# Float64 weights converted without a clamp and range-checked in a second pass, with a plan that takes transfers in the order of asking

## The chip, the cores and the metric

The kernel runs on one core of one Trainium2 chip. The metric is the device time of one execution in microseconds; lower is better. One profiled execution of the kernel before is at hand, with its trace.

## The reference

An attention block feeds a feed-forward block. For 4 batches, 8 heads, 768 steps and a head size of 48:

```python
f = 1.0 / (1.0 + np.exp(-f_logit))
for t in range(S):
    state = f[:, :, t, :, None] * state + np.einsum('bhd,bhe->bhde', k[:, :, t], v[:, :, t])
    y[:, :, t] = np.einsum('bhd,bhde->bhe', q[:, :, t], state)
x = y.transpose(0, 2, 1, 3).reshape(3072, 384)
a = x @ w1          # w1, w2: 384 x 1024
b = x @ w2
h = a * b @ w3      # w3: 1024 x 1024
out = h @ w_out     # w_out: 1024 x 384
```

q, k, v and f_logit are float32. The four weights are float64: `randn` in float32 times a Python-side `1/np.sqrt(n)`, which is a float64 number. So each weight is two 32-bit words, and the kernel makes float32 numbers of them on the chip.

## The kernel before

**Units and blocks.** The 3072 tokens are 24 units of 128 steps (6 for each batch). A unit's attention is a chunk: sigmoid gates on ACT, two scans on DVE (`fwd`, line 388, and `bwd`, line 410), the products K (418) and Q (404) on DVE, pair products on PE, a causal select on POOL (571), values and state on PE. The first four units (`u < NPE`) have a form of their own that uses PE fully for 128 steps; from unit 4 on a "visit" of PE does the values of unit u together with the pairs of unit u+1 (lines 515, 441, 534, 548). Four units make a block of 512 tokens for the feed-forward part, so there are six blocks. A unit's output `ys` (710) goes into the block's `xt`: for the first four units by PE (739, 744), for later ones through DRAM, written as `yt` (731) and gathered into `xt` (734).

**Feed-forward.** w3 @ w_out is folded into one matrix `wc` first: eight folds of 16 PE matmuls each (line 1221), copied by ACT (1228). Block 0 and half of block 1 multiply x by w1 and w2 plainly (`part`: copy `ab` on ACT, 798; product on DVE, 803). The rest uses a block product of seven multiplications (`seven`): m1, m6, m5, m2, m7, m4, m3 on PE, the copy k1 (tile `a`, line 864) of m1's result on ACT, sums on DVE (885 to 903). The down product does the same (line 997 for its sums, 1004 and 1017 for its copies on ACT). All feed-forward matmuls are issued in `three`, line 761. DVE makes differences of the weights once (1253, 1267) and of a block's xt (831).

**Weights.** `fetch` (from line 1109) loads a piece of float64 weights (line 1138) into one of a few places of the tile `place` and converts it in `sub`. With hi and lo the two words of a number:

- ACT, 1157: m = |hi|, as float32
- ACT, 1160: lo times 2^-51 plus 2, which leaves rounded bits of lo
- DVE, 1163: m clamped between LOW and HIGH
- DVE, 1164: m shifted left by 3
- DVE, 1168: sign bit of hi, or-ed with lo's bits
- DVE, 1174: the sum of the two

The clamp sends a number outside float32's useful range to an end of it. There are 12 pieces of w1 and w2 (512 columns), 4 of w_out (768), 8 of w3 (1024). A new piece may be loaded only when the DVE operation of 1168 has read the one that held the place.

**What sets the order.** Nothing is scheduled at run time. `Plan` collects tasks (engine, cost, dependencies, priority) and `order` lays them out by a list schedule: of the tasks that can start, the one that starts earliest, then the one with the lower priority number. The instructions are emitted in that order, so each engine's queue has a fixed order, and an instruction that waits holds what stands behind it. A transfer is two tasks: an issue on SP (0.45) and a task of an engine "DMA" (size over rate), made by `moves` (329). In spans where the plan sees PE idle in the first 35 us, `idle` (268) puts in filler matmuls on `floor`.

**The end.** `judge` (DVE) looks at the smallest of the gates' products and whether all outputs are numbers; the verdict goes through DRAM (1291, 1295) into the word `left`. Each engine reads it just before PE's last matmul group and, if it is set, a slower general program runs behind. For these inputs it is not set.

Of the kernel before, what the change touches and what calls it, by code (L numbers as in the profile page):

```python
# [36 lines left out]
F32 = mybir.dt.float32  # L37
# [30 lines left out]
HIGH = float.fromhex("0x1.dffffep+16")  # L68
W = C // 2
FULL = 35.0  # L70
FLOOR = 2.0**-60
RANGE = 2.0**-40


class Plan:
# [15 lines left out]

    def add(self, eng, cost, emit, deps=(), prio=0.0, takes=(), frees=(), lag=0.2, slack=0.0):


        t = {
            "eng": eng, "cost": cost, "emit": emit, "deps": [d for d in deps if d is not None], "prio": prio,
            "takes": list(takes), "frees": list(frees), "lag": lag, "slack": slack, "at": None, "end": None, "no": len(self.tasks),
        }
        self.tasks.append(t)
        return t  # L100

    def order(self):
        free, done, left = {}, [], list(self.tasks)
        enders = {}
# [15 lines left out]
        def start(t):  # L120

            waits, at = list(t["deps"]), free.get(t["eng"], 0.0)
            for name in t["takes"]:
                if name in self.pools:
                    ends = places(t, name)
                    if not ends:
                        return None
                    at = max(at, min(ends)[0])
                    continue
                n, taken = self.slots[name]  # L130
                if len(taken) >= n:
                    waits += enders[id(taken[-n])]
            ready = after(t, waits)
            return None if ready is None else max(at, ready)

        while left:
            at, _, _, t = min(
                ((at, t["prio"], t["no"], t) for t in left if (at := start(t)) is not None), key=lambda x: x[:3]
            )
            t["at"], t["end"] = at, at + t["cost"]  # L140
            free[t["eng"]] = t["end"]
            for name in t["takes"]:
                if name in self.pools:
                    t["got"] = min(places(t, name))[1]
                    self.pools[name][t["got"]] = t
                else:
                    self.slots[name][1].append(t)
            left.remove(t)
            done.append(t)
# [4 lines left out]
def kernel(  # L154
# [19 lines left out]
    with tc.manual_schedule():  # L174
        outside = ranged(tc, q, k, f_logit, v, w1, w2, w3, w_out, out, ident, w12, wc, left)
        with tc.If(outside > 0, preferred_fallthrough_block=True, label="general"):
            general(tc, q, k, f_logit, v, leaf_mask, out, ident, w12, wc)

# [6 lines left out]
def place_of(jc):  # L185

    return jc % KH * 2 + jc // KH
# [7 lines left out]
def ranged(ctx, tc, q, k, f_logit, v, w1, w2, w3, w_out, out, ident, w12, wc, left):  # L195
# [16 lines left out]
    floor = keep.tile([R, NQ], F32, name="floor")  # L212
    back = keep.tile([R, NQ], F32, name="back")
    gate = [keep.tile([R, NQ + 1], F32, name=f"gate{i}") for i in range(2)]
    qs, ks, fs = ([keep.tile([R, NQ], F32, name=f"{nm}{i}") for i in range(n)] for nm, n in (("q", 3), ("k", 2), ("f", 2)))
    masked = [keep.tile([P, 2, HP, C], F32, name=f"A{i}") for i in range(2)]
    flat = [t.rearrange("p r h c -> p (r h c)") for t in masked]
    diag = [t[:, 0 : 2 * HP * W].rearrange("p (r h c) -> p r h c", r=2, h=HP) for t in flat]
# [109 lines left out]

    def moves(n, size, rate, emit, deps, prio, late=0.0):


        for j in range(n):
            i = plan.add("SP", 0.45, (lambda: None) if j else emit, [d] if j else deps, prio - j * 1e-3, takes=["lane"], lag=0.6)
            d = i
            t = plan.add("DMA", size / n / rate, lambda: None, [i], prio - j * 1e-3, lag=1.3 + late, frees=[i])
        return t
# [5 lines left out]
    def front(u):  # L342
# [22 lines left out]

        t["lf"] = moves(2, 197, 250, load(fu, f_logit), free(2, "g"), n0 - 30)
        t["lk"] = moves(2, 197, 250, load(ku, k), free(2, "k"), n0 - 29.5)
        t["lq"] = moves(2, 197, 250, load(qu, q), free(3, "q"), n0 - 29)

# [35 lines left out]

        t["q"] = plan.add("DVE", 0.7, scale_q, [t["p"], t["lq"]] + past(u, 3, "v", "a"), n0 + 0.1)

# [11 lines left out]

        t["k"] = plan.add("DVE", 0.7, scale_k, [t["r"], t["lk"]] + past(u, 2, "a", "t"), n0)  # L420
        if u in (2, 3):
# [208 lines left out]
    def rest(u):  # L630
# [119 lines left out]
        else:  # L750
            t["z"] = moves(2, 197, 250, written, [t["y"]], n0 - 100)
            t["x"] = moves(1, 197, 250, gathered, [t["z"]] + before, n0 - 100)

# [355 lines left out]
    def fetch(loads_, a, prio, subs, deps=()):  # L1109
# [29 lines left out]

        ld = moves(1, total, 380, load, held, prio, max(0.0, 3.5 - 1.2 * load_no) if load_no < 4 * KM else 3.0)  # L1140
        asked.append(ld)
# [4 lines left out]
        def sub(c0, c1, dst, due, waits):  # L1146
# [8 lines left out]

            def magnitude():
                nc.scalar.activation(m, hi.bitcast(F32), AF.Abs)  # L1157

            def rest():
                nc.scalar.activation(lo.bitcast(F32), lo, AF.Copy, bias=2.0, scale=2.0**-51)  # L1160

            def shifted():
                nc.vector.tensor_scalar(m, m, HIGH, LOW, ALU.min, ALU.max)
                nc.vector.tensor_scalar(m.bitcast(U32), m.bitcast(U32), 3, None, ALU.logical_shift_left)

# [9 lines left out]

            past = [joins[i] for i in mine if i in joins]
            b = plan.add("ACT", 0.2 + 0.43 * w, magnitude, [ld] + past, due)
            e = plan.add("ACT", 0.2 + 0.43 * w, rest, [ld], due)
            h = plan.add("DVE", 0.32 + 0.54 * w, shifted, [b], due)
            g = plan.add("DVE", 0.16 + 0.53 * w, signed, [e, b] + list(waits), due)  # L1180
            j = plan.add("DVE", 0.16 + 0.53 * w, joined, [h, g], due - 1)
# [92 lines left out]
    where = {}  # L1274

    def judge():
        low = work.tile([R, 1], F32, name="low")
# [5 lines left out]
        nc.vector.tensor_scalar(nil, nil, 0.0, None, ALU.is_equal)  # L1283
        good = work.tile([R, 1], F32, name="good")
        nc.vector.tensor_scalar(low, low, RANGE, None, ALU.is_ge)
        nc.vector.tensor_tensor(good, low, nil, ALU.mult)
        where["good"] = good

    def told():
        where["all"] = dram.tile([R, 1], F32, name="good")  # L1290
        nc.sync.dma_start(where["all"], where["good"])

    def heard():
        row = work.tile([1, R], F32, name="row")
        nc.sync.dma_start(row, where["all"].rearrange("r one -> one r"))
        where["row"] = row
# [7 lines left out]
    for u in range(NU):  # L1304
# [11 lines left out]
        if u == NU - 1:  # L1316
            looked = plan.add("DVE", 1.0, judge, [tk[i]["y"] for i in range(NU)], -20)
            sent = moves(1, 0.4, 250, told, [looked], 0, 20.0)
            judged = plan.add("DVE", 0.2, decided, [moves(1, 0.4, 250, heard, [sent], 0, 20.0)], -20)
# [3 lines left out]
    for t in plan.order():  # L1323
# [6 lines left out]
        t["emit"]()  # L1330
    return blk[NB - 1]["outside"]


# [335 lines left out]
```

## Time and profile before

| | us |
|---|---|
| median of 3 runs | 477.67 (477.29 to 477.99) |
| the profiled execution, its own time | 482.72 |
| its span, first to last instruction | 481.0 |
| PE busy | 468.7 |
| DVE busy | 362.8 |
| ACT busy | 141.1 |
| POOL busy | 62.5 |
| mean granted clock of PE | 0.995 |

The durations used below come from the profiled execution, which took 5.05 us more than the median of the runs. The page has busy times of each engine, the span in 40 slices, the chain of work that ended last, and the costliest groups of instructions. A share of busy time is an average over stages with different limits; the views by stage and the waits say where an engine was held and by what. In the lists of waits a row reads: engine and line that waited, what released it, total us, times, longest. In the groups it reads: line, engine, operation, output from input, shape, count, then busy us and mean ns of one, then idle time before it.

PE's instruction list has one entry for a float32 matmul; the profile shows two rows for it.

### The profile page before, as it was taken

To read this page: it belongs to the slowest core of one execution; us is meant where nothing else is said; L and a number is where in the kernel's file an instruction comes from. 1 tells how busy PE (TensorE), PEld (TensorE's weight loads), DVE (VectorE), ACT (ScalarE), POOL (GpSimd) and SP (SyncE) were. 2 spreads that over 40 slices of the span, in tenths; PEclk is the share of its full clock that TensorE was granted. 3 is DMA by queue.
4 is the path that set the end of the run, shared out by engine and by line. 5 is a ranking of instruction groups with operands and counts; after the bars stand their busy time and mean duration, and the time that the engine had idled before them with its cause. 6 is when DMAs were issued, how large, how long until landed. Compare 5 with 4: busy or idle time off the path is not lost.

```text
span 481.0 us, 11341 instructions
## 1 busy us (share of the span) xinstructions
PE 468.7 (97%) x4667; PEld 400.4 (83%) x4667; DVE 362.8 (75%) x706; ACT 141.1 (29%) x310; POOL 62.5 (13%) x88
## 2 busy tenths in 40 slices
PE   8899999999999899999999999999999999999996
PEld 7788644656799688889988889988899888889995
DVE  7999699999999689899999567357653667664541
ACT  4697456462313334432432110001100110110000
POOL 9300000013303133312422100000000000000000
PEclk9999999999999899999999999999999999999999
DMA  6899277743415566446531002000111000000011
GB/s 183 269 387 236 54 278 246 260 138 100 134 50 162 163 172 169 115 132 169 148 110 46 18 18 65 34 33 2 34 33 58 9 0 1 0 1 1 34 66 37
DMA packets 36618, 50.10 MB, mean 104 GB/s; under 512 B 4546, under 2 KB 26050, under 8 KB 35538
## 3 DMA queue, kind: packets, MB, share of 16 engines
q1 hardware_dynamic: 36562, 49.33, 33.6%
q8 instruction: 37, 0.61, 0.6%
q14 instruction: 19, 0.16, 0.1%
HBM read 40.67 MB, written 8.65 MB: 103 GB/s over the span
## 4 chain that ended last, share of the span: by engine, by line
PE 73%; DVE 13%; DMA 6%; POOL 3%; issue 2%; ACT 1%; SPq 1%; DVEq 0%; POOLq 0%; ACTq 0%
PE f L761 62%; DVE place L1168 2%; PE f L1221 2%; DMA place<-in_w_dram 2%; PE py L515 2%; DVE place L1174 2%; DMA place<-in_w_out_dram 2%; PE f L455 2%; PE pa L441 2%; PE pa L548 2%; PE py L534 1%; DMA f<-in_f_logit_dram 1%; SPq L1138 1%; POOL ab L306 1%; DVE place L1253 1%
## 5 line engine op out<-in xcount | busy, mean ns | idle before, releaser
L761 PE MATMUL f<-xt,w 128*128 128x256 f32 (+1 forms) x600 | 162.8, 401 | 3.2 <-ACT gate L380 2.0
L761 PEld LDWEIGHTS f<-xt,w 128*128 128x128 f32 x600 | 114.1, 192 | 29.5 <-issue 10.0
L761 PE MATMUL f<-place 128*128 128x192 f32 (+1 forms) x504 | 112.1, 349 | 0.1
L761 PEld LDWEIGHTS f<-place 128*128 128x128 f32 x504 | 87.7, 190 | 6.2 <-DVE place L1010 0.4
L571 POOL TENSOR_SCALAR_AFFINE_SELECT A<-A 64x512 f32<-64x512 f32 (+1 forms) x44 | 40.7, 925 | 120.3 <-ACT A L565 110.5
L1221 PE MATMUL f<-place 128*128 128x384 f32 x128 | 42.8, 489 | 0.2 <-DVE place L1174 0.2
L864 ACT COPY a<-f 128x256 f32<-128x256 f32 x36 | 13.4, 373 | 93.2 <-PE f L761 78.0
L1221 PEld LDWEIGHTS f<-place 128*128 128x128 f32 x128 | 23.8, 190 | 16.5 <-DVE place L1174 0.8
L761 PE MATMUL f<-xt,place 128*128 128x256 f32 x144 | 37.3, 382 | 0.0
L761 PE MATMUL f<-wc,ab 128*128 128x192 f32 x192 | 35.2, 327 | 0.0
L761 PEld LDWEIGHTS f<-wc,ab 128*128 128x128 f32 x192 | 32.0, 190 | 0.5
L410 DVE TENSOR_TENSOR_SCAN bwd<-gate,back 112x512 f32<-112x512 f32 x24 | 30.0, 1249 | 0.8
L388 DVE TENSOR_TENSOR_SCAN fwd<-gate,floor 112x512 f32<-112x512 f32 x24 | 29.6, 1233 | 1.1 <-ACT gate L380 0.3
L761 PEld LDWEIGHTS f<-xt,place 128*128 128x128 f32 x144 | 26.6, 189 | 3.3
L888 DVE TENSOR_TENSOR place<-f,a 128x256 f32<-128x256 f32 x36 | 15.3, 424 | 18.6 <-PE f L761 18.4
L1157 ACT ACTIVATE place<-place 128x512 f32<-128x512 f32 (+2 forms) x24 | 21.3, 886 | 8.2 <-DVE w L1174 3.8
L1160 ACT ACTIVATE place<-place 128x512 f32<-128x512 uint32 (+2 forms) x24 | 21.1, 885 | 5.1 <-DMA place<-in_w_out_dram 5.1
L674 POOL TENSOR_TENSOR G<-lasts,gate 112x4 f32<-112x4 f32 x20 | 11.1, 556 | 87.3 <-ACT lasts L393 55.2
L710 ACT ACTIVATE ys<-py 112x512 f32<-112x512 f32 x20 | 11.9, 596 | 35.6 <-PE py L534 34.6
L761 PE MATMUL f<-place,w 128*128 128x256 f32 x72 | 21.4, 379 | 0.0
L899 DVE TENSOR_TENSOR ab<-f,place 128x256 f32<-128x256 f32 x36 | 15.2, 423 | 6.2 <-PE f L761 5.3
L997 DVE TENSOR_TENSOR place<-ab 128x512 f32<-128x512 f32 x24 | 16.9, 702 | 3.5 <-PE f L761 3.5
(126 smaller groups left out, 642.9 us busy)
## 6 DMA issues: line engine op xcount, KB each, us to landing
place<-in_w_dram SPq DMA_DIRECT2D x8, 1024.0 KB, 4.7
place<-in_w_dram SPq DMA_DIRECT2D x12, 512.0 KB, 9.7
out_dram<-o SPq DMA_DIRECT2D x24, 192.0 KB, 1.9
q<-in_q_dram SPq DMA_DIRECT2D x46, 96.0 KB, 2.8
vt<-in_v_dram SPq DMA_DIRECT2D x23, 192.0 KB, 3.4
k<-in_k_dram SPq DMA_DIRECT2D x44, 96.0 KB, 2.3
f<-in_f_logit_dram SPq DMA_DIRECT2D x43, 96.0 KB, 2.5
yt<-ys SPq DMA_DIRECT2D x40, 96.0 KB, 2.4
```

Of the source, the lines that this page charges most:

```text
L388: nc.vector.tensor_tensor_scan(s["P"], gate[u % 2][:, 0:NQ], floor, 0.0, ALU.mult, ALU.max)
L410: nc.vector.tensor_tensor_scan(s["R"][:, ::-1], gate[u % 2][:, NQ:0:-1], back[:, ::-1], 0.0, ALU.mult, ALU.max)
L571: nc.gpsimd.affine_select(out=a, in_=a, pattern=pattern, compare_op=ALU.is_ge, fill=0.0, base=0, channel_multiplier=-1,)
L710: nc.scalar.activation(ys, py, AF.Copy, accum_out=ysum[:, u : u + 1])
L761: nc.tensor.matmul(out_, lhsT=lhs[i], rhs=rhs[i], start=start and i == 0, stop=i == len(lhs) - 1, skip_group_check=True,)
L864: nc.scalar.copy(q["a"], q["X"])
L888: nc.vector.tensor_tensor(ups["u3", k], q["Y"], q["a"], ALU.add)
L899: nc.vector.tensor_tensor(m if which else to(tok, half), q[bank_], m, ALU.add)
L997: nc.vector.tensor_tensor(abs_[j], x, y, op)
L1157: nc.scalar.activation(m, hi.bitcast(F32), AF.Abs)
L1160: nc.scalar.activation(lo.bitcast(F32), lo, AF.Copy, bias=2.0, scale=2.0**-51)
L1221: nc.tensor.matmul(w3s["p", jc], lhsT=w3s[jc][:, kc * P : kc * P + P], rhs=wos[:, kc], start=(kc == 0), stop=(kc == KF - 1),)
```

## The change

**Conversion.** The operations of lines 1157 and 1163 are taken out. The shift reads hi itself, in which three shifts to the left drop the sign as well. Nothing is clamped any more.

**Range.** `ranges` loads all weights a second time, in 34 pieces of 128 x 512 float64 numbers (512 KB), into the two halves of the tile `A`, which the last unit's attention has left free. Each piece gets two operations on ACT over its hi words: Abs with a sum of the results, and Sign of (the absolute value - 2^-8) with a sum. DVE compares the sums with limits at the end; the verdict joins that of `judge`. Piece i's load waits for piece i-2's Sign. If a weight is out of range, `convert`, a new function, redoes all weights with the clamp before the general program; for these inputs it does not run.

**Plan.** A DMA task's priority is now the end of its issue on SP, so that transfers run in the order in which they were asked for. The plan's constants change: rates of 300 and 400 in place of 250 and 380, other lags, a factor of 1.3 or 1.6 on transfers in two spans, all engines free only from 0.6 us, another cost for some of DVE's K products, and prefetches of units 5 to 7 asked for no earlier than 22 us before they are due. These numbers reach the chip only as an order of instructions.

```diff
-    def add(self, eng, cost, emit, deps=(), prio=0.0, takes=(), frees=(), lag=0.2, slack=0.0):
+    def add(self, eng, cost, emit, deps=(), prio=0.0, takes=(), frees=(), lag=0.2, slack=0.0, since=0.0):
...
-        free, done, left = {}, [], list(self.tasks)
+        free, done, left = dict.fromkeys(("PE", "DVE", "ACT", "POOL", "SP"), BEGIN), [], list(self.tasks)
...
+        def rank(t):
+            return t["deps"][0]["end"] - 1e6 if t["eng"] == "DMA" else t["prio"]
...
-            t["at"], t["end"] = at, at + t["cost"]
+            t["at"], t["end"] = at, at + t["cost"] * slower(t, at)
...
-            i = plan.add("SP", 0.45, ..., lag=0.6)
+            i = plan.add("SP", 0.45, ..., lag=0.85, since=since)
             d = i
-            t = plan.add("DMA", size / n / rate, lambda: None, [i], prio - j * 1e-3, lag=1.3 + late, frees=[i])
+            t = plan.add("DMA", size / n / rate, lambda: None, [i], prio - j * 1e-3, lag=1.1 + late, frees=[i])
...
-        t["lf"] = moves(2, 197, 250, load(fu, f_logit), free(2, "g"), n0 - 30)
+        since = n0 - AHEAD if 4 < u < 8 else 0.0
+        t["lf"] = moves(2, 197, 300, load(fu, f_logit), free(2, "g"), n0 - 30, since=since)
...
-        ld = moves(1, total, 380, load, held, prio, max(0.0, 3.5 - 1.2 * load_no) if load_no < 4 * KM else 3.0)
+        ld = moves(1, total, 400, load, held, prio, SURE)
...
-            def magnitude():
-                nc.scalar.activation(m, hi.bitcast(F32), AF.Abs)
...
             def shifted():
-                nc.vector.tensor_scalar(m, m, HIGH, LOW, ALU.min, ALU.max)
-                nc.vector.tensor_scalar(m.bitcast(U32), m.bitcast(U32), 3, None, ALU.logical_shift_left)
+                nc.vector.tensor_scalar(m.bitcast(U32), hi, 3, None, ALU.logical_shift_left)
...
-            b = plan.add("ACT", 0.2 + 0.43 * w, magnitude, [ld] + past, due)
             e = plan.add("ACT", 0.2 + 0.43 * w, rest, [ld], due)
-            h = plan.add("DVE", 0.32 + 0.54 * w, shifted, [b], due)
-            g = plan.add("DVE", 0.16 + 0.53 * w, signed, [e, b] + list(waits), due)
+            h = plan.add("DVE", 0.16 + 0.27 * w, shifted, [ld] + past, due)
+            g = plan.add("DVE", 0.16 + 0.53 * w, signed, [e, h] + list(waits), due)
...
+        def load(i):
+            return lambda: nc.sync.dma_start(words[:, i % 2 * WIDE : (i % 2 + 1) * WIDE], seen[i].bitcast(U32))
+        def total(i):
+            a = hi[:, i % 2 * LOOK : (i % 2 + 1) * LOOK]
+            return lambda: nc.scalar.activation(a, a, AF.Abs, accum_out=sums_[:, i : i + 1])
+        def count(i):
+            a = hi[:, i % 2 * LOOK : (i % 2 + 1) * LOOK]
+            return lambda: nc.scalar.activation(a, a, AF.Sign, bias=small, accum_out=counts[:, i : i + 1])
+        for i in range(n):
+            ld = moves(1, LOOK, 400, load(i), last[:1] if i < 2 else last[i - 1 : i], 500 + i, SURE_W)
+            a = plan.add("ACT", 0.92, total(i), [ld], 500 + i)
+            last.append(plan.add("ACT", 0.95, count(i), [a], 500 + i))
+        def verdict():
+            nc.vector.tensor_scalar(sums_, sums_, LARGE, None, ALU.is_le)
+            nc.vector.tensor_scalar(counts, counts, LOOK - 0.5, None, ALU.is_ge)
+            nc.vector.tensor_tensor(sums_, sums_, counts, ALU.mult)
+            where["weights"] = small
+            nc.vector.tensor_reduce(out=small, in_=sums_, axis=AX.X, op=ALU.min)
...
+            weighed = [ranges()] if wide else []
-            looked = plan.add("DVE", 1.0, judge, [tk[i]["y"] for i in range(NU)], -20)
+            looked = plan.add("DVE", 1.0, judge, [tk[i]["y"] for i in range(NU)] + weighed, -20)
```

Read together with the fixed order, the two orders differ like this: PE, DVE, ACT, POOL and SP do the same instructions as before but for those named here, plus three filler matmuls; their order is the same up to the opening's second unit and differs from there on.

## The prediction

> **What bounds the kernel now.** I read the page first: busy shares, slices, chain.
>
> ```profile
> span 481.0 us, 11341 instructions
> ...
> PE 468.7 (97%) x4667; PEld 400.4 (83%) x4667; DVE 362.8 (75%) x706; ACT 141.1 (29%) x310; POOL 62.5 (13%) x88
> ...
> PE   8899999999999899999999999999999999999996
> ...
> DVE  7999699999999689899999567357653667664541
> ...
> PE 73%; DVE 13%; DMA 6%; POOL 3%; issue 2%; ACT 1%; SPq 1%; DVEq 0%; POOLq 0%; ACTq 0%
> ```
>
> PE is busy 97% of the span. DVE has 13% of the chain, but only in the first third, where its slices also stand at 9. A busy PE may hide slow matmuls, so I checked the rate: from 34.74 the timeline has 72 matmuls of 256 columns in 15.7 us (0.215 each), later 48 of 512 at 0.43. PE therefore runs at its rate, and only real gaps can be won. The next view cuts PE's time into stages (columns: busy us and count of PE, PEld, DVE, ACT, POOL, then clock, DMA share, GB/s).
>
> ```profile
> 34.70:77.50 42.80, 41.60 (x146) 27.25 (x146) 37.54 (x67) 24.48 (x41) 0.71 (x2) 1.00 0.68 200
> 77.50:128.30 50.80, 50.63 (x562) 31.95 (x561) 49.65 (x64) 24.80 (x40) 7.11 (x8) 1.00 0.53 172
> ...
> 158.90:161.20 2.30, 0.34 (x3) 0.04 (x1) 0.08 (x1) 1.00 (x3) 0.75 (x2) 1.00 0.47 134
> 161.20:165.40 4.20, 4.20 (x12) 3.31 (x12) 2.85 (x8) 0.37 (x1) 0.00 (x0) 0.59 0.66 189
> 165.40:277.50 112.10, 112.01 (x2207) 99.69 (x2206) 96.96 (x193) 38.73 (x102) 29.83 (x38) 1.00 0.43 118
> 277.50:440.80 163.30, 163.30 (x816) 148.02 (x815) 99.90 (x242) 17.42 (x49) 0.00 (x0) 1.00 0.07 21
> ```
>
> Two places lose time behind the opening: one inside 34.7 to 77.5, the other at 158.9, followed by 4.2 us at clock 0.59. From 277.5 on ACT is 11% busy and DMA 7%. The waits, over the whole span, then of two windows, name them:
>
> ```profile
> PE f L761 <- ACT gate L380: 2.0, 1, 2.0
> ...
> PE f L761 <- ACT ab L798: 1.2, 1, 1.2
> ```
> ```profile
> ACT place L1160 <- DMA place<-in_w_out_dram: 5.1, 1, 5.1
> ```
> ```profile
> DVE place L831 <- DMA xt<-yt: 2.6, 1, 2.6
> ```
>
> At 50.4 ACT had waited 5.1 us for the second w_out piece, and the copy `ab` (L798) that frees PE's bank stood behind it. At 159 the gate is not the cause: DVE is let go by the same late gather of xt at 161.1, 4.7 us after its issue (median of that line 2.9). It is unit 7's, the last of FFN block 1, which PE had caught up with.
>
> [...]
>
> **The change, part by part.** Prices:
>
> ```profile
> L1157 ACT ACTIVATE place<-place 128x512 f32<-128x512 f32 (+2 forms) x24 | 21.3, 886 | 8.2 <-DVE w L1174 3.8
> ```
> ```profile
> L1168 DVE SCALAR_TENSOR_TENSOR w<-place 128x512 uint32<-128x512 uint32 x12 | 9.1, 758 | 0.0
> L1160 ACT ACTIVATE place<-place 128x512 f32<-128x512 uint32 x12 | 8.2, 692 | 0.0
> L1164 DVE TENSOR_SCALAR place<-place 128x512 uint32<-128x512 uint32 x12 | 5.1, 427 | 0.4
> L1163 DVE TENSOR_SCALAR place<-place 128x512 f32<-128x512 f32 x12 | 5.0, 418 | 0.0
> ```
> ```profile
> L710 ACT ACTIVATION_READ_ACCUMULATOR ys<-py x20: 191/194/196, 113.3 to 277.3; 112x1 f32 x20
> ```
>
> (1) Clamp gone. DVE loses L1163: 12 x 0.418 + 4 x 0.548 + 8 x 0.686 = 12.7 us; ACT loses L1157, 21.3 us. The shift now reads every other word, as L1163's input was read; it stays at 0.43. All this lies before 117 us, beside a PE that runs at its rate, so by itself it is worth only what PE waits there: 1.2 us at 50.4 and 0.2 at the second fold.
>
> (2) Order. The two kernels' orders per engine show: SP's first 45 transfers are unchanged; then all four w_out pieces go out between or right behind f, k and q of unit 4; now the second to fourth stand behind the prefetches of units 5 and 6 as well. On ACT, each w_out piece's L1160 stands behind more `ab` copies. Before the first fold PE has 60 up instructions instead of 72 (each shows as two matmuls); 12 of 512 columns, 10.3 us, move behind the folds. So the first fold asks for w3's row 0 at about 65.3 (34.3, from part 3, + 48 x 0.43 + 12 x 0.86), not 77.5. Is DVE there? From 24.2 its order needs 12 pieces x 1.67 (2.12 now, less 0.45), 4 w_out x 2.3, one row of 3.15, eight `ab` products x 0.34, one x 0.6 and 1.5 for states: 37.2, so 61.4. It is, with 4 us to spare; PE then has 5.2 us per fold against DVE's 3.1 plus about 5 per attention unit. Attention visits start earlier: before block 1's first up PE has passed seven of them, unit 7's with some 25 us to spare. The stall at 159 goes: 2.0, and 1.7 for the slow clock (12 matmuls in 4.2 us instead of 2.6). The gap of 0.3 at 134.9 likely goes too. Behind the last visit stand 564 L761 instructions instead of 517: attention ends 47 x 0.38 = 18 us earlier, near 259, with its prefetches, its stores and gathers of y on SP and its selects on POOL (62.5 us busy, mostly waiting for ACT). DVE, 97.0 of 112 us busy there now, gets denser by about a twentieth of its work: late next, 0 to 3 us, taken as 0.
>
> (3) Opening. Its chain is DVE's scans, 4.8 to 24.2, without a gap over 0.3; nothing of them changes. PE gets three more filler instructions (six matmuls of 0.25), 0.5 us of which I find in nobody's idle time; in return the transpose of unit 1's outputs (L739, 1.5) moves into a gap. Walking the new order with the present durations, all units are through at about 35.6 with three ups (1.3) done: 34.3 against 34.74. Worth -0.4, bounds -2 to +1.5.
>
> (4) Range pass. 34 pieces of 512 KB: 17.8 MB more, from about 259 on. Each is an Abs and a Sign over strided words in place: 0.69 + 0.19[...]: 1.85 us, 63 us in all, on an engine that had 17.4 of 163 us. Who waits behind them is the copy k1 (`a`, L864), and PE's m2 behind that. At 288.25 k1 starts, ends at 288.62, and the two-product m2 starts at 290.15: 1.5 us of slack, more than one Abs or Sign. ACT's order mostly puts the pair right behind a k1, one pair in about 4.7 us (one block product of seven). The load of piece i waits for Sign i-2 and has two such rounds, 9.5 less 1.85 less 0.5 of issue: 7.1 us to land. The 1024 KB transfers took 4.7, so a wait is not expected; in the crowd before 40 us 512 KB took 9.7, but that traffic is gone (21 GB/s). On SP the loads stand between output stores and xt gathers; the gathers are wanted a block (some 38 us) later. DVE gets one memset, four tiny operations and two more in `judge`, under 1 us; the verdict's two small DMAs go with eight stores left, about 36 us before the final m3, against some 6 us of need. Cost 0 to 3; I take 0.4.
>
> **Sum.** 1.2 + 0.2 + 2.0 + 1.7 + 0.3 = 5.4 won, 0.4 in the opening, 0.4 lost: 5.4. The profiled execution took 482.72 (span 481.0 and 1.72 around it), so 477.3 on its scale. But the median of the runs is 477.67, 5.05 below it: either they hardly have these stalls (both hang on one DMA's landing), or everything in them is about 1% quicker. The trace can't tell; I take half, 2.7: **475.0 us**, with 472.3 and 477.3 as ends.
>
> **Rivals.**
> *Nothing left to win.* The runs without a profile already pass both stalls; opening and range pass cancel: 477.67 - 0.4 + 0.4 = 477.7. For it: 5.05 is almost the 5.4. Against: other 5-us sources are as possible.
> *Slower: the range pass holds ACT's queue.* If landing takes over 7.1 us, an Abs waits at the head of ACT's queue and k1 and PE with it: every us above costs half a us per piece, 17 us in all. If only ten pieces are late by 0.7 beyond k1's slack, it is 7 lost, 2.7 won: 482. For it: the 9.7 us row. Against: the idle DMA.
> *The opening gains more*, 3 us by smoother ACT and DVE queues: 472. Against: the scans' chain is untouched.
> *The order does not change where it matters* is excluded: SP's order differs from 31 us on.
>
> **How the numbers follow.** Main case 0.55, its own range 472 to 477; nothing left 0.20; slower 0.13; opening 0.12. A measurement here tells about 0.2% (1 us) from no change. Faster: 0.51 of the main case, the opening's 0.12, 0.05 of the second: 0.68. Same: 0.17; slower: 0.15. Range 470.8 to 478.8: it leaves out the bigger losses and a gain beyond 7.
>
> **What would show it.** Right: no L798 or xt wait of PE over 0.5 us, no half clock in mid-span, first fold near 65, last visit near 259, 34 pairs on ACT with k1's wait unchanged. Wrong: PE waiting for ACT `a` after 259, ACT waiting for DMA `A`, or new PE gaps behind DVE between 65 and 259.

## The result, and the profile after

The kernel after takes 476.11 us (median of 14 runs, 475.47 to 477.02), the kernel before beside it 477.83 (14 runs, 476.94 to 479.51): the medians differ by 1.7 us. The ratio of all runs to before's is 0.9953 (95% interval 0.9939 to 0.9967), which is about 2.2 us. The spread shrank as well: 1.6 us from lowest to highest, where before has 2.6. The profiled execution of the kernel after took 475.89, which is about its median; that of before had taken 482.72. In line numbers, after's `three` is L784 (L761 before), the copy `ab` is L821 (L798), the copy of `xt` L767 (L744), the copy k1 L887 (L864).

First the page of the kernel after: span, busy time of each engine, PE and DVE in 40 slices, the chain that ended last.

```profile
span 474.2 us, 11502 instructions
...
PE 466.2 (98%) x4673; PEld 399.6 (84%) x4673; DVE 354.6 (75%) x689; ACT 174.1 (37%) x422; POOL 64.4 (14%) x88
...
PE   7999999999999999999999999999999999999996
...
DVE  8999999999999998889945666366754667655541
...
PE 95%; DVE 2%; issue 1%; DMA 1%; ACT 0%; POOL 0%; SPq 0%; DVEq 0%; ACTq 0%
```

PE's 8 in mid-span (slice 14 of before) is gone, and the chain is PE's for 95% instead of 73%: little else is left in it. DVE is still at 9 in the first third, and no wait of PE for it is seen behind 36 us. The same by stages (us, then busy us and count of PE, PEld, DVE, ACT, POOL, clock, DMA share, GB/s):

```profile
34.70:77.50 42.80, 42.80 (x167) 30.06 (x166) 40.12 (x62) 18.21 (x29) 0.61 (x2) 1.00 0.83 267
158.90:161.20 2.30, 2.30 (x93) 2.17 (x85) 2.20 (x4) 1.48 (x4) 0.24 (x1) 1.00 0.83 228
161.20:165.40 4.20, 4.20 (x80) 3.53 (x82) 3.96 (x8) 1.50 (x5) 2.09 (x3) 1.00 0.66 192
277.50:440.80 163.30, 163.30 (x825) 148.62 (x824) 99.94 (x246) 58.55 (x158) 0.00 (x0) 1.00 0.33 107
```

The first stage has no loss left (41.60 of 42.80 before), and the two around 160 have PE busy throughout at clock 1.00 instead of 0.34 of 2.30 busy and then 0.59. In the last, ACT has 58.55 us instead of 17.42 and DMA a third of the time: the range pass is there and PE does not feel it. The four longest waits of PE over the whole span (engine, line, releaser, us, times, longest):

```profile
PE f L290 <- DVE floor L313: 1.7, 1, 1.7
PE py L478 <- DVE K L441: 0.7, 1, 0.7
PE pa L454 <- DVE Q L427: 0.5, 1, 0.5
PE f L762 <- ACT ys L733: 0.4, 1, 0.4
```

These and two more of 0.2 us each are all in the opening; behind 36 us there is none.

### The profile page after: what moved, and what is told of

Read it like the earlier page. It is cut to its first block, busy times and chain, and to the rows that moved or that the text cites. A ratio compares the mean times of both kernels' runs of the same rounds, so it can differ in the third digit from the quotient of the medians.

```text
span 474.2 us, 11502 instructions
## 1 busy us (share of the span) xinstructions
PE 466.2 (98%) x4673; PEld 399.6 (84%) x4673; DVE 354.6 (75%) x689; ACT 174.1 (37%) x422; POOL 64.4 (14%) x88
## 4 chain that ended last, share of the span: by engine, by line
PE 95%; DVE 2%; issue 1%; DMA 1%; ACT 0%; POOL 0%; SPq 0%; DVEq 0%; ACTq 0%
PE f L784 73%; PE f L1239 9%; PE py L538 3%; PE pa L464 2%; PE pa L571 2%; PE f L478 2%; PE py L557 2%; PE f L762 1%; DVE fwd L411 1%; PE f L492 1%; DVE Q L427 1%; DVE bwd L433 1%; DMA f<-in_f_logit_dram 1%; PE pa L454 0%; PE f L498 0%
## 5 line engine op out<-in xcount | busy, mean ns | idle before, releaser
L784 PE MATMUL f<-xt,w 128*128 128x256 f32 (+1 forms) x600 | 160.8, 397 | 0.0
L784 PEld LDWEIGHTS f<-xt,w 128*128 128x128 f32 x600 | 112.9, 190 | 23.9 <-issue 10.0
L784 PE MATMUL f<-place 128*128 128x192 f32 (+1 forms) x504 | 112.7, 350 | 0.0
L784 PEld LDWEIGHTS f<-place 128*128 128x128 f32 x504 | 87.6, 190 | 6.1 <-DVE place L908 0.2
L887 ACT COPY a<-f 128x256 f32<-128x256 f32 x36 | 13.4, 372 | 67.1 <-PE f L784 58.3
L784 PE MATMUL f<-xt,place 128*128 128x256 f32 x144 | 37.1, 380 | 0.0
L784 PE MATMUL f<-wc,ab 128*128 128x192 f32 x192 | 35.3, 327 | 0.0
L784 PEld LDWEIGHTS f<-wc,ab 128*128 128x128 f32 x192 | 31.9, 190 | 0.4
L784 PEld LDWEIGHTS f<-xt,place 128*128 128x128 f32 x144 | 27.0, 189 | 3.6
L1314 ACT ACTIVATE A<-A,back 128x512 f32<-128x512 f32 x34 | 26.3, 774 | 0.7
L1310 ACT ACTIVATE A<-A 128x512 f32<-128x512 f32 x34 | 23.1, 678 | 3.5 <-DMA A<-in_w_dram 3.0
L697 POOL TENSOR_TENSOR G<-lasts,gate 112x4 f32<-112x4 f32 x20 | 13.1, 657 | 79.0 <-ACT lasts L416 62.5
L784 PE MATMUL f<-place,w 128*128 128x256 f32 x72 | 21.5, 380 | 0.0
```

Source lines behind the costliest of these rows:

```text
L784: nc.tensor.matmul(out_, lhsT=lhs[i], rhs=rhs[i], start=start and i == 0, stop=i == len(lhs) - 1, skip_group_check=True,)
L887: nc.scalar.copy(q["a"], q["X"])
L1310: return lambda: nc.scalar.activation(a, a, AF.Abs, accum_out=sums_[:, i : i + 1])
L1314: return lambda: nc.scalar.activation(a, a, AF.Sign, bias=small, accum_out=counts[:, i : i + 1])
```

## The experiments

The kernel before was run again in each session; its medians there were 478.38 (first four runs), 477.73 (next four), 478.39 (next three) and 478.56 (last). Kernels that leave out the range pass say so.

**Where do the lost microseconds of before lie?** Before, once more, unchanged.

> The kernel before, profiled a second time, to see whether the two stalls of the first profile (1.2 us behind the copy ab at 50, 2.0 us and a half clock of 1.7 us at 159) belong to every execution. Theory A (they are a fixed part of it): time 482 to 483, both stalls again. Theory B (they hang on when one transfer lands, and the first profile caught a bad execution): 477 to 479.5, at most one of the two stalls and less than 2 us of PE's waits together behind the opening.

It took 479.42. PE's two longest waits behind 34 us (a third, of 0.2, is at the second fold):

```profile
PE f L761 <- ACT gate L380: 1.3, 1, 1.3
PE f L761 <- ACT ab L798: 0.2, 1, 0.2
```

The same two places as in the first profile of before (2.0 and 1.2 there), but smaller, and the first without a lower clock behind it (granted 1.00 from 156 to 164 us). So each theory has one half right: both stalls are there again, and the time is that of a better execution. The places belong to the kernel's order; the sizes belong to the execution. The way to account for them is to compare where PE's last matmul starts, with PE's gaps taken off. A gap here is the time from one matmul's start to the next beyond what is usual for that line, where it is 0.2 us or more and behind 34.5 us; before's first row includes 1.67 for the matmuls at a granted clock of 0.59.

| profiled execution | time | last matmul starts | gaps | start less gaps |
|---|---|---|---|---|
| before, first | 482.72 | 475.88 | 6.03 | 469.85 |
| before, again | 479.42 | 472.71 | 2.70 | 470.01 |
| rule only, first / again | 477.31 / 478.04 | 470.69 / 471.36 | 0.85 / 1.47 | 469.84 / 469.89 |
| clamp out, three executions | 476.70 / 476.87 / 477.61 | 470.13 / 470.03 / 470.90 | 0.69 / 0.37 / 1.52 | 469.44 / 469.66 / 469.38 |
| clamp out and rule | 477.22 | 470.66 | 1.15 | 469.51 |
| after without the rule | 477.45 | 470.88 | 1.38 | 469.50 |
| after's plan, old conversion | 482.04 | 475.33 | 4.96 | 470.37 |
| after without range pass | 476.33 | 469.57 | 0 | 469.57 |
| after | 475.89 | 469.49 | 0 | 469.49 |

The last column spans 1.0 us where the times span 6.8: these kernels differ by PE's gaps. Behind the last matmul's start another 6.4 to 6.8 us follow in each. A small part is no gap: in the last column the kernels with the clamp stand at 469.8 to 470.4 and those without it at 469.4 to 469.7, some 0.4 us less, and where that comes from was not followed. The rest of the table is explained one run at a time.

**Does the range pass cost anything?** The kernel after, with the pass left out.

```diff
-        if wide:
-            nc.vector.tensor_tensor(good, good, where["weights"], ALU.mult)
...
-            weighed = [ranges()] if wide else []
+            weighed = []
```

> The changed kernel without the range pass: the 34 loads, 68 operations on ACT and the verdict on the weights are left out, the rest of the change stays. Prediction's term: the pass costs 0.4 us (0 to 3), so 475.7, ratio to before 0.9955. Rival (the pass holds back copies on ACT and eats a good part of the gain): 473 to 474.5, ratio at most 0.992.

476.35 (6 runs, 476.24 to 476.47), ratio to before 0.9947, interval 0.9927 to 0.9968; after, in other runs, is 476.11. The 17.8 MB and 68 activations cost nothing that can be measured.

**The clamp alone.** The kernel before with the conversion of after: Abs and clamp out, the shift from hi; the old plan, but for the costs of these operations; no look at the weights.

```diff
-                nc.scalar.activation(m, hi.bitcast(F32), AF.Abs)
...
-                nc.vector.tensor_scalar(m, m, HIGH, LOW, ALU.min, ALU.max)
-                nc.vector.tensor_scalar(m.bitcast(U32), m.bitcast(U32), 3, None, ALU.logical_shift_left)
+                nc.vector.tensor_scalar(m.bitcast(U32), hi, 3, None, ALU.logical_shift_left)
...
-            b = plan.add("ACT", 0.2 + 0.43 * w, magnitude, [ld] + past, due)
...
-            h = plan.add("DVE", 0.32 + 0.54 * w, shifted, [b], due)
+            h = plan.add("DVE", 0.16 + 0.27 * w, shifted, [ld] + past, due)
```

> The kernel before with the conversion without a clamp alone (Abs on ACT and the clamp on DVE out, the plan's costs of these operations adapted); all other constants and rules of the plan as before, no range pass. In its order 60 ups stand before the first fold and 563 matmuls behind the last visit, nearly as in the changed kernel (60 and 564). Theory A (the shorter conversion lets the plan move the folds and the attention forward, and that takes the stalls away): about as fast as the changed kernel without range pass, 475 to 476.3. Theory B (the plan's new rule and constants do it): not faster than 477.

477.50 (22 runs, 476.26 to 481.52), ratio 0.9994, interval 0.9978 to 1.0009: no gain clear of noise, as Theory B has it, though the best run is as fast as after. Its order has the 60 up instructions ahead of the first fold, and the first fold at 66.6 us. So the move that the prediction's second part described comes from the clamp's removal, by way of the operations and costs that the planner no longer adds up, and in all three profiles of this kernel the stalls at 50 and 159 are gone. But the runs lie up to 5 us apart, so something else took their place in many executions.

**The plan alone.** The kernel after with the old conversion, clamp and all, and without the range pass.

> The changed kernel's plan (transfers in the order of asking, new constants) with the old conversion, clamp included, and no range pass. In its order 72 ups stand before the first fold and 501 matmuls behind the last visit. Theory A: the attention comes as late as before, the units of block 1 may hold PE as at 159; 477 to 479. Theory B (plan): 475 to 476.3.

482.2 (6 runs, 481.24 to 484.47), ratio 1.008, interval 1.0052 to 1.0107: slower, and beyond what either theory allowed. PE's largest wait in it, then DVE's instructions around it (start, us, ..., idle before and its releaser):

```profile
PE f L784 <- DVE place L1033: 3.0, 1, 3.0
```
```profile
296.70 0.43 DVE L854 TENSOR_TENSOR place<-xt 128x256 f32<-128x256 f32 x1 [4.55 <-DMA xt<-yt]
...
298.17 0.35 DVE L1033 TENSOR_TENSOR place<-f,place 128x192 f32<-128x192 f32 x1
```

The form is that of the stall at 159 in before: a sum that PE wants stands in DVE's queue behind an operation that waits for a gather of xt. The conversion and its costs are the old ones here, so what the planner has of after is the rule for transfers and the other constants. With the clamp in place, the order that they make leaves this gather too little time.

**What spreads the runs with the clamp alone?** Two more executions of it.

> The kernel before with only the clamp taken out (and the look at the weights left out), once more, for a profile of another execution, since its runs spread over 5 us. Theory A (one transfer's landing decides): an execution at 477 to 480 shows one to three gaps of PE of 0.5 to 2 us in 35 to 160 us, each behind an instruction that waits for a DMA (a w_out piece, a weight piece, or the gather of xt). Theory B (everything is a little slower, with no gap): the last matmul comes later by the same share everywhere, and no new gap over 0.3 us is seen.

> As the run before it, a third execution of the kernel before with only the clamp taken out. Theory A: gaps of PE behind a late DMA in 35 to 160 us that add up to the time above 476.3 us. Theory B: no gap, a uniform share.

476.87 and 477.61. The slower one's only wait of PE behind 34 us, and ACT's instructions there:

```profile
PE f L761 <- ACT xt L744: 1.4, 1, 1.4
```
```profile
36.33 0.69 ACT L1157 ACTIVATE place<-place 128x512 f32<-128x512 uint32 x1 [2.43 <-DMA place<-in_w_dram]
39.09 0.67 ACT L1157 ACTIVATE place<-place 128x512 f32<-128x512 uint32 x1 [2.07 <-DMA place<-in_w_dram]
39.66 0.46 ACT L744 COPY xt<-f 128x384 f32<-128x384 f32 x1
```

The copy of xt, whose input PE had finished long before, stands behind two weight pieces that wait for their transfers. The three executions show this wait at 0.2, 0.5 and 1.4 us and no other over 0.2. That agrees with Theory A for what was profiled; no execution above 477.61 was, so what makes the slowest ones (481.52) is not shown.

**The rule for transfers, taken out of after.** Everything else of after is kept, the range pass too.

```diff
         def rank(t):
-            return t["deps"][0]["end"] - 1e6 if t["eng"] == "DMA" else t["prio"]
+            return t["prio"]
```

> The kernel after, the planner's rule for DMA taken back: among tasks that could start at once a transfer is again taken by its priority instead of in the order of asking (all other new constants kept). SP's and POOL's orders stay the same, as do the counts of ups before the first fold (60 or so); in the stretch from 37 to 61 us a handful of weight shifts on ACT stand in another order against the copies `ab`, and DVE takes two `ab` products a weight piece earlier or later. Theory A (the rule's effect is only such a reshuffle, and what keeps the time narrow are the transfer prices): 476.1, within 0.6 us of the kernel after. Theory B (the rule is what keeps the order right where transfers are crowded): a wait of ACT for a w_out piece returns with a copy `ab` behind it, PE waits 0.5 to 1.5 us for `ab` near 50 us, 476.7 to 478 us, with a wide spread.

477.73 (14 runs, 476.40 to 480.41), ratio 0.999, interval 0.9974 to 1.0007. The whole gain and the narrow spread are gone, so Theory A falls. The orders do differ by only a few instructions of ACT and DVE, as was expected, and that is enough. Theory B has the time and the spread right, but not the place: PE's waits are at 40 and 44 us and not near 50. ACT in this run, then ACT in the kernel after:

```profile
37.42 0.69 ACT L1180 ACTIVATE place<-place 128x512 f32<-128x512 uint32 x1 [2.36 <-DMA place<-in_w_dram]
38.01 0.35 ACT L821 COPY ab<-f 128x256 f32<-128x256 f32 x1
39.72 0.67 ACT L1180 ACTIVATE place<-place 128x512 f32<-128x512 uint32 x1 [1.36 <-DVE S L712]
40.29 0.46 ACT L767 COPY xt<-f 128x384 f32<-128x384 f32 x1
```
```profile
36.71 0.70 ACT L1180 ACTIVATE place<-place 128x512 f32<-128x512 uint32 x1 [1.36 <-DVE place L1183]
37.30 0.47 ACT L767 COPY xt<-f 128x384 f32<-128x384 f32 x1
39.00 0.69 ACT L1180 ACTIVATE place<-place 128x512 f32<-128x512 uint32 x1 [1.23 <-DMA place<-in_w_dram]
```

The rule puts the last copy of block 0's xt ahead of one more weight piece: 37.30 against 40.29. Without it PE waits 0.8 us for xt and 0.2 for `ab`, behind another piece. (The view puts the wait of the piece at 39.72 down to DVE, and that of the one at 37.42 to its transfer.) With it, the late piece at 39.00 stands behind the copy, and delays only what has time.

**Is the rule enough, with the clamp out?** The kernel before with the clamp out (no look at the weights) and that one rule.

```diff
+        def rank(t): return t["deps"][0]["end"] - 1e6 if t["eng"] == "DMA" else t["prio"]
...
-                ((at, t["prio"], t["no"], t) for t in left if (at := start(t)) is not None), key=lambda x: x[:3]
+                ((at, rank(t), t["no"], t) for t in left if (at := start(t)) is not None), key=lambda x: x[:3]
```

> The kernel before with the clamp taken out (the look at the weights left out) and, of all the planner's changes, only the rule that takes transfers in the order of asking. PE's order is that of the run with the clamp alone; on ACT the third copy of xt (L744 there, the one whose waits PE showed in all three profiles of the clamp alone: 0.2, 0.5 and 1.4 us at 38.5) stands one 512 KB weight piece earlier, one `ab` copy and one weight piece change places, and one w_out load goes out later on SP. Theory A (that copy behind a late weight piece is what spreads the runs of the clamp alone): no wait of PE for xt at 38 to 40 us, a median of 476.3 (476.0 to 476.8), runs within 1 us of one another. Theory B (the spread has another source, such as the crowd of transfers itself, and the rule alone does not help): median 477.0 to 477.8, runs over 3 us apart.

477.87 (14 runs, 476.18 to 480.58), ratio 0.9994, interval 0.9976 to 1.0013. The wait for xt is gone, as expected (L746 there: the copy starts at 35.91 instead of 39.66), and the time is no better: Theory A falls. PE now waits elsewhere:

```profile
PE f L763 <- ACT ab L800: 0.8, 2, 0.5
```

One of these is at 40.5, where the `ab` copies stand behind a gate that waited for the load of f and behind a weight piece that waited 1.75 us; the other at 49. So the loss does not hang on one copy: with this pair in order, other pairs of a copy and a late piece still stand badly. Without the clamp, the rule fails without the other constants of after (here), and the constants fail without the rule (the run before). Which of the constants are needed was not tried, and no execution of this kernel above 477.22 was profiled.

**The rule alone, on the kernel before**, clamp and all; the edit is the one above.

> The kernel before, clamp and all, with only the rule that takes transfers in the order of asking. PE's order is that of before; one w_out load goes out on SP ahead of f and k of the next unit, and on ACT one `ab` copy comes ahead of the weight piece it stood behind. Theory A (the rule cures what hangs on a late piece near 50 us, and nothing else): PE's wait for `ab` there (1.2 and 0.2 us in the two profiles of before) goes, the wait at 158 to 160 us for the gather of xt (2.0 and 1.3 us) stays, since the order of PE is unchanged: a median 0.2 to 1.0 us below before, 477.0 to 477.8, still spread over 2 us or more. Theory B (the rule by itself is the whole gain): 476.3 or less, no gap at 158 to 160 us.

> The kernel before with the planner's rule alone, once more, for a profile of another execution: the first had no stall at 157 us where two executions of before had 1.5 and 2.1 us. Adding up so far: in every execution the last matmul starts at 469.4 to 469.9 us plus PE's gaps of over 0.2 us behind 34.5 us, and the time is 6.4 to 6.9 us more. Theory A (the stall at 157 us stands in this kernel too, whenever unit 7's gather of xt lands late, since PE's order is that of before): a gap of 0.5 to 2 us at 157 to 159 us, if the execution takes 477.5 or more. Theory B (with the w_out load moved, the stall is gone for good): no gap over 0.3 us there whatever the time, and what exceeds 477 us lies in other gaps. In both, time = 469.8 + gaps + 6.4 to 6.9, within 0.5 us.

477.64 (22 runs, 476.85 to 478.90), ratio 0.9992, interval 0.998 to 1.0005. The wait for `ab` near 50 is gone in both profiles. The stall near 158 is absent in the first (0.15 us) and back in the second, which took 478.04; PE there, then DVE's wait at the same time:

```profile
156.12 1.47 PE L763 MATMUL f<-xt,w 128*128 128x256 f32 x6
158.36 2.83 PE L763 MATMUL f<-xt,w 128*128 128x256 f32 x12 [0.76 <-ACT lasts L395]
```
```profile
DVE place L833 <- DMA xt<-yt: 1.4, 1, 1.4
```

The last up instructions of FFN block 1 have no time to spare for the gather, which took 4.5 us to land. The list of waits names ACT, as it named the gate before; DVE's wait shows the transfer. So on before the rule mends the place near 50 but not the one near 158, as Theory A of both runs has it. The second went only where the clamp was out. There PE does unit 7's visit at 126 to 128 us (clamp out, after) and not at 149 (before), which leaves its gather more time.

**Could the range pass have held ACT's queue?** The kernel after, every engine's order unchanged, with one buffer for the pieces in place of two. Only the landing budget changes, that is, the time that a load may take to land before ACT asks for its piece.

```diff
-            return lambda: nc.sync.dma_start(words[:, i % 2 * WIDE : (i % 2 + 1) * WIDE], seen[i].bitcast(U32))
+            return lambda: nc.sync.dma_start(words[:, 0:WIDE], seen[i].bitcast(U32))
...
-            a = hi[:, i % 2 * LOOK : (i % 2 + 1) * LOOK]
+            a = hi[:, 0:LOOK]
... (the same for the Sign)
```

> The kernel after, every engine's order unchanged, but the range pass's pieces all land in one buffer instead of two in turn, so the load of a piece waits for the Sign of the piece just before. Theory A (the range pass costs nothing only because its pieces land before ACT asks for them): the landing budget falls from some 5 us to what lies between one Sign and the next Abs, 3.85 (mean spacing of the pieces, 127 us over 33) less 1.85 = 2.0 us, against a landing of 3.7; so an Abs waits some 1.7 to 2.2 us at the head of ACT's queue in nearly every piece, the copy `a` (L887) behind it comes late beyond its slack of 1.5 us, and PE waits for ACT `a`: 34 pieces x 0.5 to 2.2 us = 17 to 70 us slower, 493 to 546 us, with PE waiting for ACT `a` L887 between 258 and 470. Theory B (ACT has so much idle time there, over 60%, that a late piece is made up before anybody needs `a`): within 2 us of the kernel after, 474 to 478.

527.2 (one run), 51 us slower, inside the 493 to 546 of Theory A. All of PE's waits behind 34 us:

```profile
PE f L784 <- ACT a L887: 18.3, 12, 4.2
PE f L784 <- ACT place L1027: 11.0, 3, 5.3
PE f L784 <- ACT ab L915: 6.4, 3, 2.7
```

They add up to 35.7. Behind the one shown below PE's granted clock is 0.50; over the span its mean is 0.973 instead of 0.999, and PE's busy time is 482.2 instead of 466.2: 16 more, which with the waits is about the loss. Here is one of them as ACT shows it: an Abs that waits for its piece, with a down product's copy behind it. Then follow PE's busy time and clock there by stages:

```profile
312.46 0.65 ACT L1310 ACTIVATE A<-A 128x512 f32<-128x512 f32 x1 [4.21 <-DMA A<-in_w_dram]
...
313.98 0.30 ACT L1027 COPY place<-f 128x192 f32<-128x192 f32 x1
```
```profile
309.50:314.30 4.80, 0.00 (x0) 0.00 (x0) 0.00 (x0) 1.78 (x5) 0.00 (x0) 0.83 0.43 143
314.30:317.00 2.70, 2.67 (x8) 2.67 (x9) 0.36 (x1) 0.00 (x0) 0.00 (x0) 0.50 0.62 169
```

ACT is busy for a third of this run (173.2 us). That it has idle time does not help the copy: it stands where the order put it, behind an Abs that waits 4.21 us.

**A planner that reckons with one buffer.** Each load has the Sign just before as its dependency in the plan. The expectation speaks of one buffer, but this is the only line that differs from the kernel after: the pieces still land in two buffers in turn.

```diff
-            ld = moves(1, LOOK, 400, load(i), last[:1] if i < 2 else last[i - 1 : i], 500 + i, SURE_W)
+            ld = moves(1, LOOK, 400, load(i), last[:1] if i < 1 else last[i : i + 1], 500 + i, SURE_W)
```

> The kernel after with one buffer for the pieces of the range pass, as in the run of 527.2 us, but with the planner told of it: it gives each load the Sign of the piece just before as its dependency, so it spaces the pairs on ACT at what it thinks a piece takes, 7.1 us (0.45 + 1.28 + 1.1 + 2.0 of transfer, 0.92 + 0.95 and lags), against 6.05 that a piece should need on the chip (0.5 + 3.7 + 1.85). Theory A (what costs time is an order that asks too early, not the wait as such): 476 to 480, no wait of PE for `a` L887 over 0.5 us; the pass ends near 258 + 34 x 7 = 496 in the worst case, and then the last stores, which wait for the verdict, set the end instead: up to 500. Theory B (any pass with one buffer holds ACT's queue): 500 to 530 with PE waiting for `a`, as in that run.

509.54 (one run). PE has no wait at all behind 34 us. That can't decide between the theories, since on the chip the loads do not wait as with one buffer: 29 of the 33 behind the first go out before the Sign of the piece just before has ended (one at 408.24 us, while that Sign ends at 415.41). Whether an order planned for one buffer would carry a kernel that has one was not tried. What the run does show is the price of spreading the pass: the pairs come 7.1 us apart instead of 4.0, and the time is 9.5 us beyond the upper end of Theory A, which had left out how long the verdict takes. The end of the run:

```profile
488.30 0.74 ACT L1314 ACTIVATE A<-A,back 128x512 f32<-128x512 f32 x1
...
490.94 0.33 SPq L1348 DMA_DIRECT2D good<-good  x1
...
498.23 0.30 SPq L1352 DMA_DIRECT2D row<-good  x1
...
502.85 0.36 SPq L1076 DMA_DIRECT2D out_dram<-o  x1
```

The last piece is looked at 18 us after PE's last big product, and from the last Sign to the last store's issue it is another 14.5 us: two small DMAs one after the other, 7.3 us to land the first.

## Why the prediction was right or wrong

**Only PE's gaps can be won.** Held, but for the 0.4 us of the table's last column: times that differ by 6.8 us come down to starts within 1.0. The rate that the step goes by is the one in before's trace (0.215 us for 256 columns, granted clock 1.00); that PE can't run faster was the author's assumption, and no run shows it.

**Part 1, the clamp by itself.** Held in that busy time is worth little as such: with 21.3 us off ACT and 12.7 off DVE the clamp alone has a ratio of 0.9994. The waits at 50 us and at the second fold, for which the step took 1.4 us, did go; others came. The shift reads every other word now and takes 420 ns for 512 columns (L1183 in after), where L1164 took 427, so its price held; L1163, to which the step likened it, read m and not every other word.

**Part 2, the order.** First fold at 65.8 (65.3 forecast), no clock below 1.00, no stall at 159, no new wait behind DVE. Attention ends at 250, not 259: it moved by 26.8 us. Of these, 20.4 are the 47 more instructions behind the last visit, at 0.43 us each where the step took 0.38; the other 6.4 are that the last matmul itself comes earlier than in the profiled execution of before, a gain that the sum counts and this step forgot. What the step did not have is which edit makes which move. The experiments give it: the fold, attention and both old stalls go with the clamp alone. But its order puts a new queue problem near 38.5 us in their place (with the rule added, others at 40 and 49), which no step of the prediction saw; the rule together with the other new constants takes those away, and only so was there a gain.

**Part 3, the opening.** Forecast -0.4, measured +0.1: three ups are done at the 36.12 us where PE starts on the rest, so 34.8 against 34.74. The units were through 0.5 later than walked. The walk used before's durations for the scans' chain. In the new order other products of it have POOL's select beside them (two took 1.54 and 1.60 us instead of 0.69 and 0.68, one 0.69 instead of 1.40); that this is the reason is the author's guess (see the last section).

**Part 4, the range pass.** Forecast 0.4, measured nothing: 476.11 with it, 476.35 without. The groups of the kernel after from 260 to 441 us (busy, mean ns, then idle before), and the loads' landing:

```profile
L1314 ACT ACTIVATE A<-A,back 128x512 f32<-128x512 f32 x32 | 24.8, 773 | 0.7
...
L1310 ACT ACTIVATE A<-A 128x512 f32<-128x512 f32 x32 | 21.7, 678 | 3.5 <-DMA A<-in_w_dram 3.0 <-DMA A<-in_w_out_dram 0.4
...
L1310 ACT ACTIVATION_READ_ACCUMULATOR A<-A 128x1 f32 x32 | 6.1, 191 | 0.0
```
```profile
A<-in_w_dram SPq DMA_DIRECT2D x26, 512.0 KB, 3.6
```

A pair costs 678 + 191 + 773 + 189 ns = 1.83 us, forecast 1.85. The Sign takes 95 ns more than the Abs; what the forecast had for that was an assumption of the author's, and whether the 95 belong to the function or to its bias is not shown, as no run has one function with and without a bias. The pairs come closer than the step took, every 4.0 us on average instead of 4.7, so the landing budget was about 5.6 and not 7.1 (two rounds less 1.85 and 0.5); the 3.85 in the expectation of the single buffer divides too short a stretch. The landing, 3.7 in the median with a longest of 5.2, was inside it still: the Abs waited four times, 3.5 us in all and at most 1.5, within k1's slack. (The prediction had named such waits as a sign of being wrong; here they were harmless.) The slower rival's mechanism is real, but its price was too low: with the single buffer the budget is about 2.1 us, the landing 3.8, and half a us per piece for each us above makes 29 us, where the run lost 51, 16 of them in PE's busy time (mean granted clock 0.973).

**The sum.** On profiled executions 5.4 was forecast and 6.83 measured (482.72 to 475.89). The gaps were 6.03 (the prediction's list has 5.4: it took the waits of 1.2, 0.2 and 2.0 where the gaps are 1.36, 0.34 and 2.13, and it lacked one of 0.25 at 265); the start less gaps moved by 0.36, the time behind the last matmul by 0.44, and these two were not traced further. The mis-sized term is the half: 2.7 for the median, measured 1.7. It was a guess between two readings, as the prediction says, so that the median came out within 1.1 us of the forecast is in part luck. Of the two readings of the 5.05 us, the first is the one the runs show: executions of before differ by the size of their stalls, not by pace. A usual one, at 477.83, should hold some 477.83 - 6.7 - 469.9 = 1.2 us of gaps (worked out from the table; no execution of that length was profiled); the profiled one held 6.03. Half of an unusual execution's loss was still more than a usual one's.

**The rivals.** "Nothing left to win" (477.7) missed the 476.11 by 1.6 us, the main case (475.0) by 1.1. Its reason is half right: usual executions do hold stalls, but small ones. "The opening gains more" is excluded by the 34.8.

## What to carry to other kernels

In a queue with a fixed order, ask of every instruction that waits for a transfer what stands behind it: the removal of 34 us of busy time gave nothing clear of noise while copies of half a us stood behind late pieces, and an engine two thirds idle can still be the one that is waited for (ACT with the single buffer: 33% busy, PE's waits for it 35.7 us). Read one profile's stalls for their places and several for their sizes; take PE's gaps off each execution before comparing times. Try a planner's constants and the code that they were set for together: the new plan with the old conversion was 0.8% slower, the new conversion with the old plan no faster, and both together 0.5% faster.

## What the runs showed of the hardware

**Lower clock behind a gap.** In before a gap of 2.1 us was followed by a mean granted clock of 0.59 over the next 4.2 us (1.00 in the 2.30 us that hold the gap). A gap of 1.5 us in before's second execution was not followed by one (1.00 from 156 to 164 us), nor was one of 3.1 us in the run with the plan alone (1.00 in each stage from 295 to 306 us). One of 5.0 us with the single buffer was (0.83 in the stage that holds it, then 0.50 over 2.7 us). So the length of the gap alone does not tell which is followed by a lower clock; what does, the runs do not settle.

**DVE beside POOL.** In the opening of the kernel after, a product on DVE, the next one, and the causal select on POOL:

```profile
22.59 0.69 DVE L441 TENSOR_TENSOR K<-ab,bwd 112x512 f32<-112x512 f32 x1
23.20 1.60 DVE L427 TENSOR_TENSOR Q<-place,fwd 112x512 f32<-112x512 f32 x1
```
```profile
23.16 1.09 POOL L594 TENSOR_SCALAR_AFFINE_SELECT A<-A 128x1024 f32<-128x1024 f32 x1 [5.09 <-ACT A L585]
```

Two products of one shape, 0.69 and 1.60 us: the second started with the select (23.20 and 23.16) and took 0.91 us longer, where the select took 1.09. In before the product at 22.24, with a select from 21.94 to 23.09, took 1.40 and the one at 23.56 took 0.68. Up to 25 us three DVE operations in each kernel took longer than the same operation does elsewhere, each with a select under way: by an estimate 1.7 us in before and 2.5 in after (what they took less the 0.69 or 0.36 of the same operation alone). Why the two engines hold each other up, if they do, is not shown. No run here moved the select alone, so its share of the opening's 0.5 us is read from the trace and not shown.
